# Probabilities times values in four tiles of TensorE: 64 keys against the 96 queries that see them

## The chip, the cores and the metric

The kernel runs on one core of one Trainium2 chip. The metric is the device time of one execution in microseconds (us). The time before is the median of three runs.

## The reference

A windowed attention is followed by a gated MLP. There are 8 batches and 8 heads, 576 positions and 64 numbers per head. Heads 0 to 3 see the last 32 positions (plain), heads 4 to 7 every fourth of the last 128 (dilated).

```python
scores = scale * np.matmul(q, k.transpose(0, 1, 3, 2))
rel = pos[:, None] - pos[None, :]
mask_plain = (rel >= 0) & (rel < window)                                        # window = 32
mask_dil = (rel >= 0) & (rel < window * dilation) & (rel % dilation == 0)       # dilation = 4
scores = np.where(masks[None, :, :, :], scores, -1000000000.0)
attn = np.exp(scores - np.max(scores, axis=-1, keepdims=True))
attn = attn / (np.sum(attn, axis=-1, keepdims=True) + 1e-09)
attn_out = np.matmul(attn, v)                   # (8, 8, 576, 64)
...
h = x @ w_in                                    # x: (4608, 512), w_in: (512, 2048)
g = h * (1.0 / (1.0 + np.exp(-1.702 * h)))
return g @ w_out                                # w_out: (2048, 512)
```

## The kernel before, in words

**Pairs.** Two heads of one batch make a pair, 32 pairs `k` in all, four to a batch (the first two plain, the last two dilated). The dilated heads' positions are sorted by their remainder by 4, so that in both kinds a query sees only the 32 positions before and with it. Pairs 0 to 3 have a path of their own (`first_product`). Pairs 4 to 31, 28 of them, go through `attention`: the change is there.

**One pair.** `scores` (L480) multiplies blocks of 32 queries by 64 keys in tiles of TensorE of 64 rows and 32 columns, head `a` in row group `a`, into the two banks of the PSUM tile `sp`, columns 0 to 319 of each. VectorE adds the mask (`add_mask`; for pairs below 8 TensorE does it), takes maxima and sums; ScalarE takes exponentials; GpSimd or VectorE divides by the sums. VectorE transposes blocks of 32 by 32 into `ct` (L531). Eight copies (L540 to L545, on ScalarE or VectorE, by DMA for pairs 4 to 7) lay the blocks out in `bt`, whose zeros are written once at L1180. `product` multiplies them by the values `v`; `drain_x` copies the result from PSUM to `xm`, `arena` and, for positions 512 to 575, to `rests_x`.

**The product before.** For each of nine blocks of 64 queries and each of the two heads, one matmul takes the 96 keys that the block can see (`bt` of 96 partitions, `v` of 96 by 64) and writes 64 queries. Head `a` writes to partitions 64 `a` and up, so that two column tiles are in use. Queries 0 to 511 go to the tile `av`, the last 64 to columns 320 to 383 of the second bank of the `sp` tile that holds the next pair's scores (`rest`). For pairs 24 and up a tile `sp` of its own holds both.

**The MLP.** Groups 0 to 2 (512 tokens each, one batch) run `up` (L821, into the one bank `hp_m`), a tanh on ScalarE (L829), a product on VectorE (L830), which frees `hp_m`, a split into a high and a low half (`gh`, `gl`), and `Down.pieces` (L758 to L762, `acc_m`). The other six groups run as three blocks `p`, `q`, `r` (L964, L1079) with sums of weights and tokens instead. Every matmul there is 128 by 128 by 512.

**The order.** Nothing is ordered by hand: the steps are handed to `Plan` with a cost per engine, with what they read and write (`"sp"`, `"left"`, `"av"` and so on) and an urgency. `Plan.placed` lists them engine by engine from these costs, and where a step may run on two engines it picks one. Each engine then runs its list in that order. When a cost changes, the list changes in places that are far from it too. A product is one step of TensorE; if it is `joint`, the next pair's scores stand ahead of it in the same step. DMAs are issued from the queue of SP.

**Helpers.** Copies all run at L338 (ScalarE) or L340 (VectorE), sums and differences of two tensors at L345, so that tiles tell them apart.

Of the kernel before, what the change touches and what calls it, by code (L numbers as in the profile page):

```python
# [34 lines left out]
W = 64  # L35
NW = 9
KW = 96
ROW = S // 4
INNER = 24
# [176 lines left out]
def tile_windowed_attention_then_gated_mlp(  # L216
# [41 lines left out]
    ghs, gls = ([fixed([P, GT], F32R, f"{n}{j}") for j in range(2)] for n in ("gh", "gl"))  # L258
    bt = fixed([P, 2, NW + 1, D], F32, "bt")
    arena = fixed([P, NU, GT], F32, "arena")  # L260
# [22 lines left out]

    cts = [fixed([P, 2, 2, QT, 32], F32, f"ct{j}") for j in range(2)]

    third = area(13, 3)
    prs.append(third[:, 0:2 * QT * W].rearrange("p (a t w) -> p a t w", a=2, t=QT))
    cts.append(third[:, 2 * QT * W:4 * QT * W].rearrange("p (h a t q) -> p h a t q", h=2, a=2, t=QT))

# [36 lines left out]
    def mask_dilated():  # L326

        A.activation(mask, plain, AF.Copy)
        G.affine_select(out=mask[0:32, 1, 0:48], in_=mask[0:32, 1, 0:48], pattern=[[0, 48]], compare_op=ALU.is_ge,
                        fill=NEG, base=15, channel_multiplier=-1)  # L330
        V.memset(mask[32:64, 1, 0:16], NEG)
        V.memset(mask[32:64, 2, 0:32], NEG)
        A.activation(mask[32:64, 3], mask[0:32, 1], AF.Copy)
        V.memset(mask[64:96, 3, 0:16], NEG)

# [15 lines left out]
    def decode(n, urgency):  # L351
# [21 lines left out]
        def fetch(e):  # L373
            if n == 3:
                raw = bt.rearrange("p a n w -> p (a n w)")[:, 0:2 * DM].bitcast(U64)
            else:
                raw = temp([P, DM], U64, "qk", f"cell_{n}") if n == 4 else cells[r]
            at["halves"] = raw.bitcast(U16).rearrange("p (n t) -> p n t", t=4)
            at["low"], at["top"] = (raw.bitcast(U32).rearrange("p (n t) -> p n t", t=2)[:, :, j] for j in range(2))
            load(raw, src)  # L380
# [21 lines left out]
    late, main_x, left_x = area(0, 4), area(9, 4), left  # L402
    nv = NW * D
    pairs = [{} for _ in range(B * NC)]
# [23 lines left out]
    def load_v(k):  # L428
        u, place = pairs[k], lots(k)[1]

        def work(e):
            if k < NC:
                n = (QT if dilated(k) else QT + 1) * 2 * D
                flat = (None, late, main_x, left_x)[k][:, 2 * S:2 * S + n] if k else temp([P, n], F32, "v", f"v_{k}")
                u["v"] = flat.rearrange("p (s a d) -> p s a d", a=2, d=D)

                load(flat, first_v[k][:, 2 * D * (QT + 1) - n:])
                return
            flat = temp([P, 2 * nv], F32, "v", f"v_{k}")
            u["v"] = [flat[:, nv * a:nv * a + nv].rearrange("p (m d) -> p m d", m=NW) for a in range(2)]  # L440
            for a in range(2):
                load(u["v"][a][0:KW], vp[k - NC, :, a])

        add({DMA: 390 if k < NC else 442}, (-6.7, -6.7, -3.8, -1.6)[k] if k < NC else 1.6 * k - 0.3, work, waits(k),
            (place, place + "l"), (0.0, 4.0, 11.0, 14.0)[k] if k < NC else 0.0)
# [15 lines left out]
    def scores(k):  # L461
# [8 lines left out]
        for t in range(QT):  # L470
            for a, g in [(a, g) for a in range(2) for g in range(4 if k < NC or t < QT - 1 else 2)]:
                rows = slice(D * a, D * a + D)
                dst = u["box"][a][32 * g:32 * g + 32, t]
                at = ROW * g + 32 * t if k < NC else P * t + 32 * g

# [36 lines left out]
    def softmax(k, urgency):  # L512
# [10 lines left out]
        if k < NC:  # L523

            for a in range(2):
                to = ct.rearrange("p h a t q -> p (h a t q)")[:, a * QT * W:a * QT * W + QT * W]
                add({DVE: 0.48}, urgency, lambda e, a=a, to=to: V.transpose(
                    out=to, in_=pr[:, a].rearrange("p t w -> p (t w)")), (PR, f"{PR}.{a}"), (f"{CT}.{a}",))
            return
        for half in (0, 1):  # L530
            add({DVE: 0.42}, urgency, lambda e, half=half: V.transpose(  # L531
                out=ct[:, half], in_=pr[:, :, :, 32 - 32 * half:64 - 32 * half]),
                (PR, f"{PR}.0", f"{PR}.1"), (f"{CT}.{half}",))
# [3 lines left out]
        for m in range(8):  # L537
            j, prev = m % 4, m // 4
            row = 32 * (j % 2) + (0 if prev else 32)
            dst = bt[row:row + 32, :, j // 2::2, 32 * (j % 2):32 * (j % 2) + 32]  # L540
            src = ct[32 * j:32 * j + 32, prev]

# [9 lines left out]
    def first_product(k):  # L552
# [4 lines left out]
        u = pairs[k]  # L557
        ct = cts[turn(k)].rearrange("p h a t q -> p (h a t q)").rearrange("p (a n) -> p a n", a=2)
        u["x"] = first_x[:, :, ROW * (k % 2):ROW * (k % 2) + ROW]
# [13 lines left out]
    def product(k):  # L573
        u = pairs[k]
        if k < INNER:
            u["av"] = bank([P, GT], "av", f"av_{k}")
            n = following(k)
            sp = pairs[n]["sp"] if n else bank([P, 2, GT], "sp", f"rest_{k}")
            u["rest"] = sp[:, 1, QT * W:QT * W + LT]
        else:  # L580
            sp = bank([P, 2, GT], "sp", f"av_{k}")
            u["av"], u["rest"] = sp[:, 0], sp[:, 1, 0:LT]
        for m in range(NW):
            for a in range(2):
                rows = slice(D * a, D * a + D)
                dst = u["av"][rows, D * m:D * m + D] if m < NW - 1 else u["rest"][rows]
                T.matmul(dst, u["v"][a][0:KW, m], bt[0:KW, a, m], start=True, stop=True, skip_group_check=True)

    def drain_x(k, urgency):
# [7 lines left out]

        if dilated(k) and b:
            def whole():
                return u["av"][:, 0:432].rearrange("p (r i) -> p r i", r=3)  # L600
            mains = [(384, lambda x: x[:, 0:3], lambda: whole()[:, :, 0:P], False),
                     (80, lambda x: x[:, 3, 0:80], lambda: u["av"][:, 432:512], False),
                     (48, lambda x: x[:, 3, 80:P], lambda: u["rest"][:, 0:48], True)]
            rests = [(lambda x: x[:, 0:3], lambda: whole()[:, :, P:], False),
                     (lambda x: x[:, 3], lambda: u["rest"][:, 48:], True)]
        else:
            mains = [(GT, lambda x: x, lambda: u["av"], False)]
            rests = [(lambda x: x, lambda: u["rest"], True)]
        if b == 0:
# [26 lines left out]
        if b >= ALONE:  # L636
            add({DMA: 262}, urgency, lambda e: load(tokens_x[k], to), [f"{name}.{n}" for n in range(3)], (f"tx{k}",))
        for n, (part, src, other) in enumerate(rests):
# [5 lines left out]
    def store_rest(b, c, urgency):  # L644
        if c < NC - 1:
            return
        y = 1 - b % 2
        dst = tokens_r.rearrange("c p (b n) -> b p c n", b=B)[b]
        add({DMA: 66}, urgency, lambda e: load(dst, rests_x[:, y]), [f"xr{y}{i}.{n}" for i in range(NC) for n in range(2)],
            (f"tr{b}",))  # L650

    def parts(k):
        return 3 if dilated(k) else 1

# [10 lines left out]
    def attention(k, urgency):  # L665
# [25 lines left out]
        def work(e):  # L691
# [5 lines left out]
        places = ("sp",) if k >= INNER else ("left", "av", "sp") if joint else ("left", "av")  # L697
        add({PE: 2.2 if joint else 1.25}, urgency - 1.0e5, work,
            (lots(k)[1], *(f"bt.{m}" for m in range(8)), *need), places, 1.0)
# [12 lines left out]
    def unit(i):  # L712
        if i < NU:
            return arena[:, i]
        if i >= NU + 4:
# [6 lines left out]
            if n >= 8:  # L722
                return bt.rearrange("p a n w -> p (a n w)")[:, GT * (n - 8):GT * (n - 7)]
            if n < 6:
                return prs[n - 4].rearrange("p a t w -> p (a t w)")[:, 0:GT]
            return cts[n - 6].rearrange("p h a t q -> p (h a t q)")[:, 0:GT]
        if "wi_last" not in misc:
# [62 lines left out]
    class Group:  # L790
# [366 lines left out]
    for i, name in enumerate(("qk0", "qk0", "v0", "v0", "pr0", "pr1", "ct0", "ct1")):
# [106 lines left out]
```

## Time and profile before

| what | value |
|---|---|
| median of three runs | 838.21 us (837.95 to 838.41) |
| profiled execution | 835.92 us, span 834.2 us |
| mean granted clock of TensorE | 0.993 |
| first and last record of the changed product (L587) | 71.8 and 472.0 us |
| DMA, whole span | 191.47 MB, mean 230 GB/s |

The span runs from the first to the last instruction; the rest of an execution lies outside. Line numbers are those of the kernel before. In the profile an f32 matmul of the program is two records on PE and two weight loads on PEld. The shape behind a matmul (96\*64, 64\*32) is the rows and columns of its tile. Ends of matmul records are modelled, so their starts are what is read.

### The profile page before, as it was taken

Reading aid. Unit: us, or ns where it says so; the run is one execution under the profiler, and the core shown is the slowest. Engines: PE = TensorE matmul, PEld = TensorE weight load, DVE = VectorE, ACT = ScalarE, POOL = GpSimd, SP = SyncE. Lnnn points to the kernel's source line nnn. Section 1 sums busy time; section 2 is a strip of 40 time slices with the busy share of each in tenths; the row PEclk is TensorE's granted clock in tenths of the full one; section 3 lists DMA queues with packets and bytes.
Section 4 is the critical chain, followed back from the end, with each engine's and each line's share of the span. In section 5 each row is a group of like instructions: output and inputs, shape, how many; then the busy total and the mean of one; then the engine's idle time right before and its main releaser. Section 6 shows DMA issues by size and latency. Waiting matters only on the chain. (4 is left out here: it accounts for less than half of the span.)

```text
span 834.2 us, 18369 instructions
## 1 busy us (share of the span) xinstructions
PE 817.4 (98%) x7016; PEld 659.3 (79%) x7016; DVE 682.0 (82%) x1104; ACT 521.5 (63%) x936; POOL 331.2 (40%) x296
## 2 busy tenths in 40 slices
PE   7899999999999999999999999999999999999997
PEld 4578887888887888787888887888888888888886
DVE  6898999878889977887988999886678976767575
ACT  7898876776777666767765764445446544544340
POOL 3443235566754565234322463541125431112251
PEclk9899999999999999999999999999999999999999
DMA  9477659999867747859777877685655658665546
GB/s 359 144 250 221 196 155 301 297 294 315 272 216 249 231 153 235 285 191 320 245 235 253 252 251 243 218 272 178 208 182 192 202 190 264 227 187 170 200 144 185
DMA packets 113128, 191.47 MB, mean 230 GB/s; under 512 B 28176, under 2 KB 57104, under 8 KB 113040
## 3 DMA queue, kind: packets, MB, share of 16 engines
q1 hardware_dynamic: 112896, 190.16, 70.2%
q8 instruction: 56, 0.92, 0.5%
q14 instruction: 32, 0.26, 0.1%
q10 hardware_dynamic: 144, 0.13, 0.0%
HBM read 143.85 MB, written 45.09 MB: 226 GB/s over the span
## 5 line engine op out<-in xcount | busy, mean ns | idle before, releaser
L345 POOL TENSOR_TENSOR arena<-arena 128x256 f32<-128x256 f32 (+3 forms) x102 | 108.8, 1072 | 118.2 <-DVE wi_last_units L345 23.0
L821 PE MATMUL hp_m<-xs,wi_kept 128*128 128x512 f32 x504 | 129.2, 398 | 1.5 <-DVE arena L830 1.0
L821 PEld LDWEIGHTS hp_m<-xs,wi_kept 128*128 128x128 f32 x504 | 92.8, 188 | 24.0 <-DVE arena L830 3.1
L338 ACT ACTIVATE wo_kept<-arena 128x512 fp32r<-128x512 f32 x111 | 69.4, 630 | 41.9 <-PE second_r_Q L1079 10.0
L964 PE MATMUL up_r<-wi_kept,xs 128*128 128x512 f32 x336 | 85.4, 389 | 0.0
L964 PE MATMUL up_p<-wi_kept,xs 128*128 128x512 f32 x336 | 85.0, 395 | 0.2 <-DVE arena L986 0.2
L964 PE MATMUL up_q<-wi_kept,xs 128*128 128x512 f32 x336 | 83.5, 389 | 0.3 <-DVE arena L986 0.3
L345 POOL TENSOR_TENSOR wo_kept<-arena,wo_kept 128x512 fp32r<-128x512 f32 x32 | 43.0, 1349 | 93.2 <-ACT wo_kept L338 50.9
L964 PEld LDWEIGHTS up_q<-wi_kept,xs 128*128 128x128 f32 x336 | 63.0, 188 | 13.8 <-DVE arena L986 0.7
L964 PEld LDWEIGHTS up_p<-wi_kept,xs 128*128 128x128 f32 x336 | 62.0, 188 | 14.5 <-DVE arena L986 0.6
L964 PEld LDWEIGHTS up_r<-wi_kept,xs 128*128 128x128 f32 x336 | 63.1, 188 | 13.1
L345 DVE TENSOR_TENSOR wo_kept<-arena,wo_kept 128x512 fp32r<-128x512 f32 x89 | 67.8, 770 | 6.4 <-ACT wo_kept L338 5.8
L345 POOL TENSOR_TENSOR wo_kept<-wi_last_units,wo_kept 128x512 fp32r<-128x512 f32 x25 | 34.7, 1388 | 94.7 <-ACT wo_kept L338 90.3
L338 ACT ACTIVATE bt<-ct 32x320 f32<-32x320 f32 x124 | 58.2, 469 | 14.2 <-DVE ct L531 10.4
L345 POOL TENSOR_TENSOR pr<-pr,sm 128x320 f32<-128x320 f32 x52 | 43.7, 857 | 54.6 <-DVE sm L510 45.2
L758 PE MATMUL acc_m<-gh,wo_kept 128*128 128x512 f32 x156 | 61.4, 394 | 0.3 <-ACT arena L338 0.3
L759 PE MATMUL acc_m<-gh,wo_kept 128*128 128x512 f32 x156 | 60.8, 389 | 0.0
L985 ACT ACTIVATE arena<-arena 128x512 f32<-128x512 f32 x60 | 37.5, 629 | 34.8 <-DVE arena L345 28.8
L345 DVE TENSOR_TENSOR arena<-arena 128x512 f32<-128x512 f32 (+1 forms) x71 | 55.3, 780 | 1.3 <-ACT arena L338 0.9
L345 DVE TENSOR_TENSOR gl<-arena,gh 128x512 fp32r<-128x512 f32 x54 | 46.7, 864 | 6.6 <-ACT gh L338 3.7
L338 ACT ACTIVATE wo_kept<-wi_last_units 128x512 fp32r<-128x512 f32 x48 | 30.2, 630 | 29.0 <-PE second_r_Z L1079 8.9
L338 ACT ACTIVATE gh<-arena 128x512 fp32r<-128x512 f32 x56 | 35.7, 637 | 17.8 <-DVE arena L830 6.1
(262 smaller groups left out, 1836.5 us busy)
## 6 DMA issues: line engine op xcount, KB each, us to landing
xs<-sums SPq DMA_DIRECT2D x168, 256.0 KB, 3.5
out_weights<-sums_o SPq DMA_DIRECT2D x63, 512.0 KB, 3.8
qk<-qk_dram SPq DMA_DIRECT2D x29, 576.0 KB, 4.8
v<-vp_dram SPq DMA_DIRECT2D x56, 216.0 KB, 4.2
xs<-sums_o SPq DMA_DIRECT2D x21, 512.0 KB, 3.7
sums<-arena SPq DMA_DIRECT2D x32, 256.0 KB, 3.7
sums_o<-arena SPq DMA_DIRECT2D x32, 256.0 KB, 3.6
arena<-wi_dram SPq DMA_DIRECT2D x15, 512.0 KB, 4.3
```

Of the source, the lines that this page charges most:

```text
L338: A.activation(dst, src, AF.Copy, scale=scale)
L345: (V if e == DVE else G).tensor_tensor(out=dst, in0=a, in1=b, op=op)
L758: T.matmul(self.acc[j], w[:, 0, cols], high, start=f == 0, stop=False)
L759: T.matmul(self.acc[j], w[:, 1, cols], high, start=False, stop=False)
L821: T.matmul(hps[f], wi(f)[:, st, cols], mv[:, c], start=c == 0 and k == 0, stop=c == NC - 1 and k == 2)
L964: T.matmul(self.banks[place], xs[:, slot, at:at + P], wi_kept[:, 2 * a + c, mv], start=fresh and c == 0 and k == 0, stop=c == 1 and k == 2 ...
L985: add({ACT: 0.60}, -10.0, lambda e: A.activation(unit(tmp), src(), AF.Tanh, scale=0.851), need, own(tmp))
```

## The change

- **Blocks.** Queries and keys are cut differently. A half is 320 positions, five blocks of 64; the first starts at position 0, the second at 256 for the keys. A block of 64 keys is multiplied by the up to 96 queries that see it. Lower keys (row group 0) hold the first half, upper keys (row group 1) the second, and each has two heads, so four tiles of 64 by 64.
- **Banks.** Each query is seen from two key blocks, so its two parts are added up in PSUM: only the first matmul to each bank and head has `start`. Row group 0 writes 320 columns of `av`. Row group 1 writes the 192 columns behind the scores in the first bank of `sp`, and the last 64 behind those of the second.
- **Drains.** A plain pair has two main copies and one of the rest, a dilated one five and three (before: one and one, three and two).
- **Values.** `v` is one transfer of 128 by 640 f32 instead of two of 96 by 576.
- **Around it.** The tiles of queries in `scores`, the masks, `ct` (tile ahead of head) and the eight copies to `bt` follow the new layout; five of these move 256 elements per partition and three 320 (before: eight of 320). The zeros are written over 128 by 960 instead of 96 by 1280.
- **Plan's costs.** TensorE's step is given as 1.95 and 1.05 instead of 2.2 and 1.25, the load of `v` as 328 instead of 442.

```diff
-NW = 9
+NB = 5
 KW = 96
+HALF = 2 * NB * 32
...
+    bt_all = fixed([P, 5 * 2 * P], F32, "bt")
+    bt = bt_all[:, 0:2 * NB * KW].rearrange("p (s a w) -> p s a w", a=2, s=NB)
...
-            flat = temp([P, 2 * nv], F32, "v", f"v_{k}")
-            u["v"] = [flat[:, nv * a:nv * a + nv].rearrange("p (m d) -> p m d", m=NW) for a in range(2)]
-            for a in range(2):
-                load(u["v"][a][0:KW], vp[k - NC, :, a])
+            flat = temp([P, 2 * NB * D], F32, "v", f"v_{k}")
+            u["v"] = flat.rearrange("p (a s d) -> p a s d", a=2, s=NB)
+            load(flat, vp[k - NC])
...
-                at = ROW * g + 32 * t if k < NC else P * t + 32 * g
+                at = ROW * g + 32 * t if k < NC else HALF * (g // 2) + W * t + 32 * (g % 2)
...
-                out=ct[:, half], in_=pr[:, :, :, 32 - 32 * half:64 - 32 * half]),
+                out=ct[:, half].rearrange("p t a q -> p a t q"), in_=pr[:, :, :, 32 - 32 * half:64 - 32 * half]),
...
-            row = 32 * (j % 2) + (0 if prev else 32)
-            dst = bt[row:row + 32, :, j // 2::2, 32 * (j % 2):32 * (j % 2) + 32]
-            src = ct[32 * j:32 * j + 32, prev]
+            odd, upper = j % 2, j // 2
+            row = D * upper + 32 * (odd != prev)
+            col = 32 * odd if not prev or odd else 64
+            shift = prev and not odd
+            tiles = slice(1 if shift and not upper else 0, QT - upper)
+            to = slice(1, QT) if upper and not shift else slice(0, tiles.stop - tiles.start)
+            dst = bt[row:row + 32, to, :, col:col + 32]
+            src = ct[32 * j:32 * j + 32, prev, tiles]
...
-            u["rest"] = sp[:, 1, QT * W:QT * W + LT]
+            u["x"] = u["av"][:, 0:HALF], sp[:, 0, QT * W:], sp[:, 1, QT * W:QT * W + LT]
...
-            u["av"], u["rest"] = sp[:, 0], sp[:, 1, 0:LT]
-        for m in range(NW):
-            for a in range(2):
-                rows = slice(D * a, D * a + D)
-                dst = u["av"][rows, D * m:D * m + D] if m < NW - 1 else u["rest"][rows]
-                T.matmul(dst, u["v"][a][0:KW, m], bt[0:KW, a, m], start=True, stop=True, skip_group_check=True)
+            u["x"] = sp[:, 0, 0:HALF], sp[:, 1, 0:GT - HALF], sp[:, 1, GT - HALF:S - HALF]
+        begun = set()
+        for m in range(NB):
+            for r in range(2):
+
+                n = KW if m < NB - 1 else W
+                if r == 0:
+                    spans = [(0, n, 0, W * m)]
+                elif m == 0:
+                    spans = [(W, KW, 1, 0)]
+                elif m < NB - 2:
+                    spans = [(0, n, 1, W * (m - 1))]
+                else:
+                    spans = [(0, W, 1, P), (W, KW, 2, 0)] if m == NB - 2 else [(0, W, 2, 0)]
+                for first, last, i, at in spans:
+                    bank_ = i if k < INNER else min(i, 1)
+                    for a in range(2):
+                        rows, keys = slice(D * a, D * a + D), slice(D * r, D * r + D)
+                        T.matmul(u["x"][i][rows, at:at + last - first], u["v"][keys, a, m], bt[keys, m, a, first:last],
+                                 start=(bank_, a) not in begun, stop=True, tile_position=(D * r, D * a),
+                                 skip_group_check=True)
+                        begun.add((bank_, a))
...
+        if dilated(k):
+            mains = [(2 * P, lambda y: y[:, 0:2], lambda: two(x(0, 0, 2 * ROW))[:, :, 0:P], 0),
+                     (32, lambda y: y[:, 2, 0:32], lambda: x(0, 2 * ROW, HALF), 0),
+                     (96, lambda y: y[:, 2, 32:P], lambda: x(1, 0, 96), 1),
+                     (80, lambda y: y[:, 3, 0:80], lambda: x(1, 112, 192), 1),
+                     (48, lambda y: y[:, 3, 80:P], lambda: x(2, 0, 48), 1)]
+            rests = [(lambda y: y[:, 0:2], lambda: two(x(0, 0, 2 * ROW))[:, :, P:], 0),
+                     (lambda y: y[:, 2], lambda: x(1, 96, 112), 1), (lambda y: y[:, 3], lambda: x(2, 48, LT), 1)]
         else:
-            mains = [(GT, lambda x: x, lambda: u["av"], False)]
-            rests = [(lambda x: x, lambda: u["rest"], True)]
+            mains = [(HALF, lambda y: y[:, 0:HALF], lambda: x(0, 0, HALF), 0),
+                     (GT - HALF, lambda y: y[:, HALF:], lambda: x(1, 0, GT - HALF), 1)]
+            rests = [(lambda y: y, lambda: x(2, 0, LT), 1)]
...
-        add({PE: 2.2 if joint else 1.25}, urgency - 1.0e5, work,
+        add({PE: 1.95 if joint else 1.05}, urgency - 1.0e5, work,
...
-            add({POOL: 1.2}, 20.0, lambda e: G.memset(bt[0:KW], 0.0), (), ("bt", "btl", *zeroed))
+            add({POOL: 1.2}, 20.0, lambda e: G.memset(bt, 0.0), (), ("bt", "btl", *zeroed))
```

More of the change, by code (lines that the diff above doesn't have):

```diff
@@ L258, in tile_windowed_attention_then_gated_mlp @@
     ghs, gls = ([fixed([P, GT], F32R, f"{n}{j}") for j in range(2)] for n in ("gh", "gl"))
-    bt = fixed([P, 2, NW + 1, D], F32, "bt")
+    bt_all = fixed([P, 5 * 2 * P], F32, "bt")
+    bt = bt_all[:, 0:2 * NB * KW].rearrange("p (s a w) -> p s a w", a=2, s=NB)
     arena = fixed([P, NU, GT], F32, "arena")
@@ L282, in tile_windowed_attention_then_gated_mlp @@
     sms = [fixed([P, 2, QT], F32, f"sm{j}") for j in range(3)]
-    cts = [fixed([P, 2, 2, QT, 32], F32, f"ct{j}") for j in range(2)]
+    cts = [fixed([P, 2, QT, 2, 32], F32, f"ct{j}") for j in range(2)]
     third = area(13, 3)
     prs.append(third[:, 0:2 * QT * W].rearrange("p (a t w) -> p a t w", a=2, t=QT))
-    cts.append(third[:, 2 * QT * W:4 * QT * W].rearrange("p (h a t q) -> p h a t q", h=2, a=2, t=QT))
+    cts.append(third[:, 2 * QT * W:4 * QT * W].rearrange("p (h t a q) -> p h t a q", h=2, a=2, t=QT))
     four = tc.tile_pool(name="four", bufs=1, space=bass.MemoryType.PSUM)
@@ L328, in mask_dilated @@
         A.activation(mask, plain, AF.Copy)
-        G.affine_select(out=mask[0:32, 1, 0:48], in_=mask[0:32, 1, 0:48], pattern=[[0, 48]], compare_op=ALU.is_ge,
+        G.affine_select(out=mask[0:32, 2, 0:48], in_=mask[0:32, 2, 0:48], pattern=[[0, 48]], compare_op=ALU.is_ge,
                         fill=NEG, base=15, channel_multiplier=-1)
[L331 to L334, printed above, removed]
+        V.memset(mask[32:64, 2, 0:16], NEG)
+        V.memset(mask[32:64, 4, 0:32], NEG)
+        A.activation(mask[96:128, 1], mask[0:32, 2], AF.Copy)
+        V.memset(mask[64:96, 2, 0:16], NEG)
     def copy(e, dst, src, scale=1.0):
@@ L374, in fetch @@
             if n == 3:
-                raw = bt.rearrange("p a n w -> p (a n w)")[:, 0:2 * DM].bitcast(U64)
+                raw = bt_all[:, 0:2 * DM].bitcast(U64)
             else:
@@ L402, in tile_windowed_attention_then_gated_mlp @@
     late, main_x, left_x = area(0, 4), area(9, 4), left
-    nv = NW * D
     pairs = [{} for _ in range(B * NC)]
@@ L438, in work @@
                 return
-            flat = temp([P, 2 * nv], F32, "v", f"v_{k}")
-            u["v"] = [flat[:, nv * a:nv * a + nv].rearrange("p (m d) -> p m d", m=NW) for a in range(2)]
-            for a in range(2):
-                load(u["v"][a][0:KW], vp[k - NC, :, a])
-        add({DMA: 390 if k < NC else 442}, (-6.7, -6.7, -3.8, -1.6)[k] if k < NC else 1.6 * k - 0.3, work, waits(k),
+            flat = temp([P, 2 * NB * D], F32, "v", f"v_{k}")
+            u["v"] = flat.rearrange("p (a s d) -> p a s d", a=2, s=NB)
+            load(flat, vp[k - NC])
+        add({DMA: 390 if k < NC else 328}, (-6.7, -6.7, -3.8, -1.6)[k] if k < NC else 1.6 * k - 0.3, work, waits(k),
             (place, place + "l"), (0.0, 4.0, 11.0, 14.0)[k] if k < NC else 0.0)
@@ L525, in softmax @@
             for a in range(2):
-                to = ct.rearrange("p h a t q -> p (h a t q)")[:, a * QT * W:a * QT * W + QT * W]
+                to = ct.rearrange("p h t a q -> p (h t a q)")[:, a * QT * W:a * QT * W + QT * W]
                 add({DVE: 0.48}, urgency, lambda e, a=a, to=to: V.transpose(
@@ L557, in first_product @@
         u = pairs[k]
-        ct = cts[turn(k)].rearrange("p h a t q -> p (h a t q)").rearrange("p (a n) -> p a n", a=2)
+        ct = cts[turn(k)].rearrange("p h t a q -> p (h t a q)").rearrange("p (a n) -> p a n", a=2)
         u["x"] = first_x[:, :, ROW * (k % 2):ROW * (k % 2) + ROW]
@@ L596, in view, with x, two @@
             return x.rearrange("p (i r) -> p r i", r=4) if dilated(k) and b else x
[L598 to L605, printed above, removed]
-        else:
-            mains = [(GT, lambda x: x, lambda: u["av"], False)]
-            rests = [(lambda x: x, lambda: u["rest"], True)]
+        def x(i, first, last):
+            return u["x"][i][:, first:last]
+        def two(ap):
+            return ap.rearrange("p (r i) -> p r i", r=2)
+        if dilated(k):
[6 more added lines that the diff above has]
+                     (lambda y: y[:, 2], lambda: x(1, 96, 112), 1), (lambda y: y[:, 3], lambda: x(2, 48, LT), 1)]
+        else:
+            mains = [(HALF, lambda y: y[:, 0:HALF], lambda: x(0, 0, HALF), 0),
+                     (GT - HALF, lambda y: y[:, HALF:], lambda: x(1, 0, GT - HALF), 1)]
+            rests = [(lambda y: y, lambda: x(2, 0, LT), 1)]
         if b == 0:
@@ L636, in drain_x @@
         if b >= ALONE:
-            add({DMA: 262}, urgency, lambda e: load(tokens_x[k], to), [f"{name}.{n}" for n in range(3)], (f"tx{k}",))
+            add({DMA: 262}, urgency, lambda e: load(tokens_x[k], to), [f"{name}.{n}" for n in range(5)], (f"tx{k}",))
         for n, (part, src, other) in enumerate(rests):
@@ L648, in store_rest @@
         dst = tokens_r.rearrange("c p (b n) -> b p c n", b=B)[b]
-        add({DMA: 66}, urgency, lambda e: load(dst, rests_x[:, y]), [f"xr{y}{i}.{n}" for i in range(NC) for n in range(2)],
+        add({DMA: 66}, urgency, lambda e: load(dst, rests_x[:, y]), [f"xr{y}{i}.{n}" for i in range(NC) for n in range(3)],
             (f"tr{b}",))
-    def parts(k):
-        return 3 if dilated(k) else 1
     def first_attention(k, urgency):
@@ L722, in unit @@
             if n >= 8:
-                return bt.rearrange("p a n w -> p (a n w)")[:, GT * (n - 8):GT * (n - 7)]
+                return bt_all[:, GT * (n - 8):GT * (n - 7)]
             if n < 6:
                 return prs[n - 4].rearrange("p a t w -> p (a t w)")[:, 0:GT]
-            return cts[n - 6].rearrange("p h a t q -> p (h a t q)")[:, 0:GT]
+            return cts[n - 6].rearrange("p h t a q -> p (h t a q)")[:, 0:GT]
         if "wi_last" not in misc:
@@ L803, in split_x @@
                 x = xm[:, c]
-                need = [f"xm{c}.{n}" for n in range(parts(c))]
+                need = [f"xm{c}.{n}" for n in range(5)]
                 add({ACT: 0.53}, -8.0, lambda e, hi=hi, x=x: copy(e, hi, x), need, (f"xh{c}",))
@@ L1145, in tile_windowed_attention_then_gated_mlp @@
     for c in range(NC):
-        legacy[9 + c] = tuple(f"xm{c}.{n}" for n in range(3)) + ("first v2", "first qk2")
+        legacy[9 + c] = tuple(f"xm{c}.{n}" for n in range(5)) + ("first v2", "first qk2")
         legacy[13 + c] = ("first v3", "first qk3")
@@ L1150, in tile_windowed_attention_then_gated_mlp @@
             legacy[13 + c] += tuple(f"{n}2{i}" for n in ("pr", "ct") for i in ("", ".0", ".1")) + ("mx2",)
-    legacy[16] = tuple(f"xr{y}{c}.{n}" for y in range(2) for c in range(NC) for n in range(2))
+    legacy[16] = tuple(f"xr{y}{c}.{n}" for y in range(2) for c in range(NC) for n in range(3))
     legacy[17] = ("g32",)
@@ L1155, in tile_windowed_attention_then_gated_mlp @@
     for i in (8, 9):
-        legacy[i] += tuple(f"A{i}.{n}" for n in range(3))
+        legacy[i] += tuple(f"A{i}.{n}" for n in range(5))
     for i, name in enumerate(("qk0", "qk0", "v0", "v0", "pr0", "pr1", "ct0", "ct1")):
@@ L1243 @@
     first = np.ascontiguousarray(first.reshape(NC, 2, 4, QT + 1, 32, D).transpose(0, 2, 4, 3, 1, 5))
-    vp = np.stack([vp[:, :, D * m:D * m + KW] for m in range(NW)], axis=2)
-    vp = np.ascontiguousarray(vp.reshape(B * NC, 2, NW, KW, D).transpose(0, 3, 1, 2, 4))
+    vp = np.stack([vp[:, :, 32 + first:32 + first + HALF] for first in (0, S - HALF)], axis=2)
+    vp = vp.reshape(B * NC, 2, 2, NB, W, D).transpose(0, 2, 4, 1, 3, 5)
+    vp = np.ascontiguousarray(vp).reshape(B * NC, P, 2 * NB * D)
     wi = np.asarray(inputs["moe_w_in"]).view(np.uint64).reshape(NC, P, NF, P).transpose(2, 1, 0, 3)
```

## The prediction

> **What bounds the kernel now.** I read the page first, then the busy time by stage, then what TensorE waits for in the stages that hold the change, and last the order of time around one product.
>
> ```profile
> span 834.2 us, 18369 instructions
> PE 817.4 (98%) x7016; PEld 659.3 (79%) x7016; DVE 682.0 (82%) x1104; ACT 521.5 (63%) x936; POOL 331.2 (40%) x296
> ```
>
> TensorE is busy for 98% of the span. A busy TensorE need not be at its peak, so the stages come next (columns: window, its length, then busy time and count of PE, PEld, DVE, ACT and POOL, the granted clock, the DMA share, GB/s).
>
> ```profile
> 18.00:71.00 53.00, 48.81 (x650) 36.22 (x651) 47.02 (x85) 47.52 (x74) 23.55 (x22) 0.92 0.60 193
> 71.00:125.00 54.00, 54.00 (x561) 43.21 (x561) 51.40 (x87) 46.18 (x77) 14.55 (x13) 1.00 0.69 205
> 125.00:225.00 100.00, 98.99 (x1326) 79.39 (x1326) 85.77 (x144) 70.66 (x138) 64.08 (x64) 1.00 0.91 297
> 225.00:325.00 100.00, 99.73 (x1181) 81.33 (x1176) 84.57 (x146) 69.97 (x142) 57.48 (x62) 1.00 0.65 207
> 325.00:425.00 100.00, 98.87 (x918) 79.08 (x916) 85.57 (x145) 72.57 (x138) 31.91 (x27) 1.00 0.79 263
> 425.00:475.00 50.00, 50.00 (x392) 40.56 (x379) 43.12 (x75) 32.67 (x68) 18.27 (x15) 1.00 0.78 252
> 475.00:834.00 359.00, 353.82 (x1555) 291.00 (x1553) 273.72 (x399) 168.87 (x287) 115.80 (x82) 1.00 0.64 207
> ```
>
> All 28 changed products lie between 71 and 475 us. There TensorE is busy 401.6 of 404 us at clock 1.00, VectorE 350.4 and ScalarE 292.1. The waits of TensorE in that window are few:
>
> ```profile
> PE hp_m L821 <- DVE arena L830: 2.0, 4, 1.0
> PE acc_m L758 <- ACT arena L338: 0.3, 1, 0.3
> PE up_p L964 <- DVE arena L986: 0.2, 1, 0.2
> ```
>
> That is 2.5 us in 404. So a microsecond less for TensorE there is close to a microsecond of the kernel, as long as the others keep up; after 475 us it is again TensorE (353.8 of 359).
>
> **The product, removed and added.** One joint step in order of time, TensorE alone (start, length, line, what, count), and one lone product:
>
> ```profile
> 158.94 0.97 PE L480 MATMUL sp<-qk 64*32 64x64 f32 x72
> 159.84 1.15 PE L587 MATMUL av<-bt,v 96*64 96x64 f32 x32
> 160.82 0.29 PE L587 MATMUL sp<-bt,v 96*64 96x64 f32 x4
> 161.04 2.33 PE L821 MATMUL hp_m<-xs,wi_kept 128*128 128x512 f32 x9
> ...
> 470.96 1.27 PE L587 MATMUL av<-bt,v 96*64 96x64 f32 x36
> 472.16 0.73 PE L964 MATMUL up_p<-wi_kept,xs 128*128 128x512 f32 x2
> ```
>
> An f32 matmul of the program shows as two records, which I call halves. A product is 18 matmuls, 36 halves, and holds TensorE from its first half to the next work: 161.04 - 159.84 = 1.20 us, and 472.16 - 470.96 = 1.20 us. The last six halves to `av` start from 160.65 on, the first to `sp` at 160.82:
>
> ```profile
> 160.65 0.35 PE L587 MATMUL av<-bt,v 96*64 96x64 f32 x6
> ```
>
> So two heads in two column tiles take one step of 0.17 / 3 = 0.057 us for a half each; over the whole, 32 halves in 0.98 us with the start, I use 0.058. With 18 steps per tile, 17 intervals make 0.99, and 1.20 - 0.99 = 0.21 us is start and drain.
>
> What makes the step? Windows at the beginning of the scores (PE and PEld with counts of records that fall in each) show it:
>
> ```profile
> 158.93:158.99 0.06, 0.05 (x8) 0.05 (x12) 1.00 0.43 154
> 158.99:159.02 0.03, 0.03 (x8) 0.03 (x16) 1.00 0.19 68
> 159.02:159.09 0.07, 0.07 (x18) 0.07 (x26) 1.00 0.22 73
> ...
> L480 PEld LDWEIGHTS sp<-qk x2100: 102/106/173, 5.4 to 441.1; 64*32 64x32 f32 x191
> L821 PEld LDWEIGHTS hp_m<-xs,wi_kept x504: 186/188/333, 26.9 to 330.3; 128*128 128x128 f32 x168
> L587 PEld LDWEIGHTS av<-bt,v x928: 132/138/138, 71.8 to 472.0; 96*64 96x64 f32 x186
> ```
>
> The first eight halves start at once, one in each of eight tiles of 64 rows and 32 columns; no half starts between 158.99 and 159.02, while weight loads go on; the ninth comes 0.08 us after the first. A weight load grows by (188 - 106) / 96 = 0.85 ns per column, so 32 columns are 0.027 and the 64-wide stream behind them about 0.053, or 0.83 ns per query. Two things follow. Tiles of two row groups and several column groups run beside each other, each at its own pace. And a half of 96 queries should take 96 x 0.83 = 0.080 plus the 0.005 that the step of 0.058 has over its 0.053: 0.085 us. A half of 64 or 32 queries keeps 0.058, since its weights still have 64 columns (64 x 0.85 = 0.054).
>
> The new product has 22 matmuls, 44 halves. On TensorE, the product of pair 9 and its neighbours; `av` and `sp` are PSUM tiles, `bt` the probabilities, `v` the values, `hp_m` the MLP. Before:
>
> ```order
> L480 MATMUL sp_12_2098<-qk_12_2027 32x64 x36
> L587 MATMUL av_9_2135<-bt_77,v_9_2030 64x64 x16
> L587 MATMUL sp_12_2098<-bt_77,v_9_2030 64x64 x2
> L821 MATMUL hp_m1_4_2094<-xs_72,wi_kept_68 128x512 x9
> L758 MATMUL acc_m1_3_1949<-gh0_73,wo_kept_70 128x512
> ```
>
> And now:
>
> ```order
> L482 MATMUL sp_12_2120<-qk_12_2048 32x64 x36
> L607 MATMUL av_9_2157<-bt_77,v_9_2052 64x96 x2
> L607 MATMUL sp_12_2120<-bt_77,v_9_2052 64x32 x2
> L607 MATMUL av_9_2157<-bt_77,v_9_2052 64x96 x2
> L607 MATMUL sp_12_2120<-bt_77,v_9_2052 64x96 x2
> L607 MATMUL av_9_2157<-bt_77,v_9_2052 64x96 x2
> L607 MATMUL sp_12_2120<-bt_77,v_9_2052 64x96 x2
> L607 MATMUL av_9_2157<-bt_77,v_9_2052 64x96 x2
> L607 MATMUL sp_12_2120<-bt_77,v_9_2052 64x64 x2
> L607 MATMUL sp_12_2120<-bt_77,v_9_2052 64x32 x2
> L607 MATMUL av_9_2157<-bt_77,v_9_2052 64x64 x2
> L607 MATMUL sp_12_2120<-bt_77,v_9_2052 64x64 x2
> ```
>
> The lower 64 keys go to `av`, the upper 64 to `sp`, two heads each: four tiles. A lower tile has 8 halves of 96 and 2 of 64: its nine intervals are 8 x 0.085 + 0.058 = 0.74. An upper tile has 4 of 32, 4 of 96 and 4 of 64: eleven intervals, 4 x 0.085 + 7 x 0.058 = 0.75, and it starts two issue slots later (0.01). With the same 0.21 for start and drain a product takes 0.97 us. Gain: 0.23 a product, **28 x 0.23 = 6.4 us**. The bounds: if the weight load alone sets every step, 11 x 0.058 + 0.22 = 0.86, a gain of 9.5 us; if the four tiles go key block by key block, each block as slow as its slower tile (three of 0.17, then four halves of 0.058, then two, less the last interval: 0.80), 1.02, a gain of 5.0. I take 6.4, since the tiles of the scores do not wait for each other. Issue is no limit: the first product of pair 3 sends 80 halves over eight tiles in 35.38 - 34.37 = 1.01 us, 0.013 each, and 44 of them make 0.56.
>
> ```profile
> 34.37 1.08 PE L568 MATMUL first_x<-ct,arena 32*64 32x64 f32 x80
> 35.38 0.50 PE L821 MATMUL hp_m<-xs,wi_kept 128*128 128x512 f32 x1
> ```
>
> **The other edits.** The drains are cut finer, since the result now lies in three stretches. A plain pair has one more copy, a dilated one three more.
>
> ```profile
> L338 ACT ACTIVATE arena<-av x59: 198/371/875, 73.0 to 473.2; 128x512 f32<-128x512 f32 x14, 128x384 f32<-128x384 f32 x14, 128x80 f32<-128x80 f32 x14, 128x48 f32<-128x48 f32 x10
> L338 ACT ACTIVATE arena<-sp x21: 200/253/312, 73.5 to 321.2; 128x48 f32<-128x48 f32 x10, 128x16 f32<-128x16 f32 x6, 128x64 f32<-128x64 f32 x5
> ...
>   DVE pr L345: 1.5, 3
> ...
> L338 ACT ACTIVATE bt<-ct x124: 454/470/475, 151.2 to 467.9; 32x320 f32<-32x320 f32 x124
> ```
>
> At 0.20 to 0.31 us for a small copy, 14 + 3 x 14 = 56 more copies are 11 to 17 us, fewer as the large ones shrink. Five of the eight copies into `bt` fall from 320 to 256 elements: between nothing and a fifth of 0.47 us each, 0 to 11 us over 24 pairs. ScalarE so gets between nothing and 17 us more work, in 404 us of which it idles 112. VectorE's transposes keep their count and size and only write in another layout; I cost that at nothing, under the 54 us that VectorE idles. The values come as one transfer of 327 KB in place of two of 216 KB; TensorE waits for none of them now, so I cost that at nothing, and at nothing too if the cover went, as the new transfer is smaller. The planner, given shorter costs, also lays the whole program out anew.
>
> What I do charge is one new kind of wait. The `sp` tile holds the next pair's scores, which VectorE reads, and now also 192 + 64 columns of the product, not 64. ScalarE already waits for VectorE's mask addition there, 1.5 us in three times (the row `DVE pr L345` above, of what ended the idle time before the copies out of `sp`).
>
> On ScalarE behind the product of pair 10 (`bt`, `av`, `sp` as above, `hp_m` the tanh, `pr` the exponentials, `gh` the gate). Before:
>
> ```order
> L338 ACTIVATE arena_78<-av_10_2272 128x3x128
> L338 ACTIVATE bt_77<-arena_78 32x10x32 x8
> L829 ACTIVATE arena_78<-hp_m1_6_2301 128x512
> L338 ACTIVATE arena_78<-av_10_2272 128x80
> L338 ACTIVATE arena_78<-sp_13_2235 128x48
> ```
>
> And now:
>
> ```order
> L342 ACTIVATE arena_78<-sp_13_2264 128x96
> L856 ACTIVATE arena_78<-hp_m1_6_2331 128x512
> L342 ACTIVATE arena_78<-sp_13_2264 128x80
> L342 ACTIVATE arena_78<-sp_13_2264 128x48
> L342 ACTIVATE arena_78<-av_10_2301 128x32
> L506 ACTIVATE pr1_84<-pr1_84 128x640
> ```
>
> A copy out of `sp` now stands ahead of the tanh. Whoever delays it delays the tanh, then VectorE's L830, then the next `hp_m`. The present cost of that path is the 2.0 us above; I add **0.6 us**, a guess between -1.5 (the new layout loses most of the waits of now) and +4 (it doubles them and more).
>
> Sum: -6.4 + 0.6 = -5.8 us. The profiled execution took 835.92 us (span 834.2), so 830.1; the median of the runs is 838.21, 2.29 above it, so **832.4 us**.
>
> **The rivals.**
> Waits eat the gain (slower). VectorE adds the masks in two pieces, 0.69 and 0.27 us; if ScalarE stands before that in each of the 20 pairs from 4 to 23 and half of the 0.96 reaches `hp_m`, that is 20 x 0.5 = 10 us, and 838.2 - 6.4 + 10 = 842. It decides once the delay exceeds what TensorE has in hand, the 12 matmuls of the down part (one every 0.22, 2.6 us) less tanh and L830 (0.60 and 0.69). For it: VectorE is at 86% there, and ScalarE's eight `bt` copies make 3.9 us in one piece. Against: 1.3 us in hand each time, and only four waits of now reach TensorE.
>
> ```profile
> L829 ACT ACTIVATE arena<-hp_m x48: 574/598/703, 39.3 to 346.0; 128x512 f32<-128x512 f32 x48
> L830 DVE SCALAR_TENSOR_TENSOR arena<-arena,hp_m x48: 630/687/690, 40.6 to 347.0; 128x512 f32<-128x512 f32 x48
> ...
> 157.72 0.39 PE L758 MATMUL acc_m<-gh,wo_kept 128*128 128x512 f32 x1
> 157.94 0.39 PE L759 MATMUL acc_m<-gh,wo_kept 128*128 128x512 f32 x1
> ...
> 172.26 3.85 ACT L338 ACTIVATE bt<-arena 32x320 f32<-32x320 f32 x8
> L345 DVE TENSOR_TENSOR arena<-sp,mask x6: 272/474/692, 150.7 to 283.6; 128x512 f32<-128x512 f32 x3, 64x128 f32<-64x128 f32 x3
> ```
>
> The tiles take turns (slower). If halves start only in program order, the second half of a matmul holds up the next tile, and each of the 22 matmuls costs one step: 12 x 0.085 + 10 x 0.058 + 0.21 = 1.81, +0.61 a product, +17 us: 855. Against it stand the scores: 36 matmuls in 159.84 - 158.94 = 0.90 us, where turns of 0.058 would need 2.1. [...]
>
> Half the gain: blocks in step (5.0) with +2 to +3 of waits, or 6.4 with +4: 835 to 836.3. And the weight load sets all steps: 838.2 - 9.5 + 0.6 = 829.3.
>
> **How the numbers follow.** Four tiles at their own pace with waits about as now: 0.68, which is the forecast. Half the gain: 0.15. Weight load: 0.04. Waits eat all of it and no more: 0.05. Waits eat more: 0.04; turns: 0.04. A measurement of this kernel tells 0.2% (1.7 us) from no change, so faster has 0.68 + 0.15 + 0.04 = 0.87, same 0.05, slower 0.08. The range goes from the weight-load case, 829.3, to the upper end of half the gain, 836.3; it leaves out some 0.17.
>
> **What would show it.** Right: a product from first half to next work at 0.94 to 1.02 us, 44 halves; TensorE's waits between 71 and 475 us under 5 us; everything after the last product about 6 us earlier. Wrong: a product at 1.2 us or more (turns), or `hp_m` waiting for L830 by 6 us or more, with ScalarE's copies out of `sp` waiting for the mask additions.

## The result and the profile after

| | before | changed |
|---|---|---|
| median | 837.95 us (836.90 to 838.41, 5 runs) | 830.17 us (828.89 to 830.57, 5 runs) |
| profiled execution | 835.92 us, span 834.2 us | 828.89 us, span 827.2 us |
| product, first half to next work | 1.20 us | 0.955 us |
| last product: next work starts at | 472.16 us | 465.37 us |

The ratio is 0.9905 (95% interval 0.9891 to 0.9920): 7.8 us faster, 6.7 to 9.1 by the interval. The forecast was 832.4 us in a range of 829.3 to 836.3. Line numbers are now those of the changed kernel: L607 is the product, L482 the scores, L856 the tanh and L857 VectorE's step behind it.

The page after, and the stages between 71 and 475 us and behind (columns as before):

```profile
span 827.2 us, 18837 instructions
PE 811.2 (98%) x7240; PEld 653.5 (79%) x7240; DVE 669.7 (81%) x1104; ACT 515.0 (62%) x992; POOL 327.8 (40%) x296
...
71.00:125.00 54.00, 53.91 (x602) 42.25 (x608) 47.75 (x84) 47.15 (x92) 16.73 (x14) 1.00 0.64 198
125.00:225.00 100.00, 99.40 (x1423) 80.04 (x1423) 85.27 (x151) 65.65 (x143) 62.24 (x65) 1.00 0.87 288
225.00:325.00 100.00, 99.88 (x1229) 80.70 (x1223) 80.51 (x144) 72.49 (x167) 54.04 (x59) 1.00 0.64 211
325.00:425.00 100.00, 98.41 (x915) 78.84 (x920) 88.07 (x147) 71.34 (x148) 31.81 (x28) 1.00 0.79 253
425.00:475.00 50.00, 49.35 (x468) 39.87 (x455) 44.52 (x73) 33.48 (x76) 21.81 (x19) 1.00 0.81 262
475.00:827.00 352.00, 347.10 (x1528) 286.18 (x1526) 265.73 (x394) 163.90 (x277) 112.08 (x79) 1.00 0.64 206
```

TensorE's share stays at 98%. It is busy for 98% or more of each of these stages, so it still sets the time there, and its busy time fell by 6.2 us. What it waits for between 71 and 475 us:

```profile
PE up_p L991 <- DVE arena L349: 1.3, 2, 0.7
PE up_p L991 <- DVE arena L1013: 0.9, 1, 0.9
PE acc_m L785 <- ACT arena L342: 0.3, 1, 0.3
PE hp_m L848 <- DVE arena L857: 0.2, 1, 0.2
```

2.7 us against 2.5 before, in other places: `hp_m` waits 0.2 us for VectorE, not 2.0. The product of pair 9 in order of time, TensorE alone (start, length, what, count; two halves start together, 0.007 us apart, which I read as one for each head):

```profile
157.84 0.30 PE L607 MATMUL av<-bt,v 64*64 64x96 f32 x2
157.85 0.30 PE L607 MATMUL sp<-bt,v 64*64 64x32 f32 x4
157.97 0.25 PE L607 MATMUL av<-bt,v 64*64 64x96 f32 x2
157.99 0.28 PE L607 MATMUL sp<-bt,v 64*64 64x96 f32 x2
158.05 0.25 PE L607 MATMUL av<-bt,v 64*64 64x96 f32 x2
158.10 0.25 PE L607 MATMUL sp<-bt,v 64*64 64x96 f32 x2
158.13 0.25 PE L607 MATMUL av<-bt,v 64*64 64x96 f32 x2
158.18 0.25 PE L607 MATMUL sp<-bt,v 64*64 64x96 f32 x2
158.22 0.25 PE L607 MATMUL av<-bt,v 64*64 64x96 f32 x2
158.26 0.25 PE L607 MATMUL sp<-bt,v 64*64 64x96 f32 x2
...
158.64 0.22 PE L607 MATMUL sp<-bt,v 64*64 64x64 f32 x2
158.79 0.50 PE L789 MATMUL acc_m<-gl,wo_kept 128*128 128x512 f32 x1
```

A lower tile starts a half of 96 queries every 0.08 us (157.97, 158.05, 158.13, 158.22), and an upper tile does the same in between: four tiles run beside each other. From 157.84 to 158.79 the product takes 0.95 us. So do 27 of the 28; behind one, at 168.16 us, the next work waits 0.2 us for VectorE (the `hp_m` row above). The last product, of pair 31, says the same:

```profile
464.42 1.02 PE L607 MATMUL av<-bt,v 64*64 64x96 f32 x44
465.37 0.73 PE L991 MATMUL up_p<-wi_kept,xs 128*128 128x512 f32 x2
```

Up to there the profiled execution is 472.16 - 465.37 = 6.8 us ahead; at the end it is 7.0. The products give 28 x (1.198 - 0.955) = 6.8 us.

### The profile page after: what moved, and what is told of

It is laid out like the page before. It is cut to its first block, busy times and chain, and to the rows that moved or that the text cites. A ratio compares the mean times of both kernels' runs of the same rounds, so it can differ in the third digit from the quotient of the medians.

```text
span 827.2 us, 18837 instructions
## 1 busy us (share of the span) xinstructions
PE 811.2 (98%) x7240; PEld 653.5 (79%) x7240; DVE 669.7 (81%) x1104; ACT 515.0 (62%) x992; POOL 327.8 (40%) x296
## 4 chain that ended last, share of the span: by engine, by line
PE 88%; DVE 7%; ACT 1%; issue 1%; DMA 1%; SPq 0%; DVEq 0%; ACTq 0%
PE hp_m L848 15%; PE up_q L991 9%; PE up_r L991 9%; PE up_p L991 8%; PE second_q_Q L1106 5%; PE second_r_Q L1106 5%; PE second_p_Q L1106 5%; PE acc_m L785 5%; PE acc_m L789 5%; PE acc_m L786 4%; PE sp L482 3%; PE second_r_Z L1106 3%; PE second_R L1106 3%; PE second_q_Z L1106 3%; PE second_p_Z L1106 2%; PE av L607 2%
## 5 line engine op out<-in xcount | busy, mean ns | idle before, releaser
L349 POOL TENSOR_TENSOR arena<-arena 128x256 f32<-128x256 f32 (+3 forms) x109 | 118.0, 1091 | 155.7 <-DVE wi_last_units L349 34.7
L342 ACT ACTIVATE wo_kept<-arena 128x512 fp32r<-128x512 f32 x115 | 71.9, 629 | 42.3 <-PE second_r_Q L1106 11.4
L349 POOL TENSOR_TENSOR wo_kept<-arena,wo_kept 128x512 fp32r<-128x512 f32 x34 | 45.3, 1340 | 105.5 <-ACT wo_kept L342 72.2
L349 DVE TENSOR_TENSOR wo_kept<-arena,wo_kept 128x512 fp32r<-128x512 f32 x87 | 65.3, 761 | 5.9 <-ACT wo_kept L342 5.4
L349 POOL TENSOR_TENSOR wo_kept<-wi_last_units,wo_kept 128x512 fp32r<-128x512 f32 x23 | 31.9, 1388 | 84.6 <-ACT wo_kept L342 84.6
L342 ACT ACTIVATE bt<-ct 32x256 f32<-32x256 f32 (+1 forms) x127 | 55.2, 435 | 3.2 <-DVE ct L533 0.9
L349 DVE TENSOR_TENSOR gl<-arena,gh 128x512 fp32r<-128x512 f32 x53 | 44.9, 847 | 9.1 <-PE acc_m L789 6.4
L349 DVE TENSOR_TENSOR arena<-arena 128x512 f32<-128x512 f32 (+1 forms) x68 | 50.4, 747 | 0.4
L1013 DVE SCALAR_TENSOR_TENSOR arena<-arena 128x512 f32<-128x512 f32 x60 | 48.1, 807 | 0.7 <-ACT arena L1012 0.2
```

Of the source, the lines that this page charges most:

```text
L342: A.activation(dst, src, AF.Copy, scale=scale)
L349: (V if e == DVE else G).tensor_tensor(out=dst, in0=a, in1=b, op=op)
L1013: add({DVE: -0.70 if need[0][0] == "A" else 0.70}, -10.0, lambda e: V.scalar_tensor_tensor(out=unit(dst), in0=unit(tmp), scalar=1.0, in1=s ...
```

## The experiments

Each was timed in rounds with the kernel before on the same chip; the medians of before were 837.39, 837.62 and 837.71 us in the three sets.

**The plan's costs of before in the changed kernel.**

```diff
-        add({PE: 1.95 if joint else 1.05}, urgency - 1.0e5, work,
+        add({PE: 2.2 if joint else 1.25}, urgency - 1.0e5, work,
...
-        add({DMA: 390 if k < NC else 328}, (-6.7, -6.7, -3.8, -1.6)[k] if k < NC else 1.6 * k - 0.3, work, waits(k),
+        add({DMA: 390 if k < NC else 442}, (-6.7, -6.7, -3.8, -1.6)[k] if k < NC else 1.6 * k - 0.3, work, waits(k),
```

> The changed kernel with the plan's costs of before (2.2 and 1.25 for TensorE's step, 442 for the load of the values); the work is the same, only the order of the lists may differ. Tiles theory (the gain is TensorE's time in the product, 28 x 0.243 = 6.8 us, and nothing else): the product stays at 0.955 us and the time at 830.2 us, give or take 1.5 for the other order. Plan theory (a part of the gain is the new order that the new costs made): 833 us or more with the same product.

830.25 us (ratio 0.9918, 0.9896 to 0.9940), product 0.955 us. That is 7.1 us less than the kernel before on the same chip (5.0 to 8.7 by the interval): most of the gain, if not all, does not need the new costs.

**The plan's new costs alone, in the kernel before.** The same two edits the other way round.

> The kernel before with the plan's costs of the change (1.95 and 1.05, 328) and nothing else of it. Tiles theory: the product stays at 1.198 us and the time at 838 us, give or take 1.5. Plan theory: 835 us or less, with the old product.

835.43 us (ratio 0.9976, 0.9965 to 0.9986), product 1.198 us. Neither theory had this: a new order alone made the kernel before 2.0 us faster.

**Other costs in the kernel before.**

```diff
-        add({PE: 2.2 if joint else 1.25}, urgency - 1.0e5, work,
+        add({PE: 2.1 if joint else 1.2}, urgency - 1.0e5, work,
```

> The kernel before with the plan's costs of TensorE's step at 2.1 and 1.2 (what its trace shows) instead of 2.2 and 1.25. The product stays at 1.198 us. Scatter theory (a new order moves the time by up to 2 us either way, without a trend): 835.5 to 839 us. If the costs of before were simply too high, so that lower ones gain: near 835.4 us, as with 1.95 and 1.05.

839.27 us (ratio 1.0023, 1.0011 to 1.0035), a touch above the stated band: 1.6 us slower, with costs of TensorE's step that lie between those of before and the new ones (the cost of loading `v` stays at 442 here). These two tries show no trend with the cost. A new order of the same work moved the kernel before by 2.0 us one way and by 1.6 the other.

**Measured costs in the changed kernel.**

```diff
-        add({PE: 1.95 if joint else 1.05}, urgency - 1.0e5, work,
+        add({PE: 1.85 if joint else 0.95}, urgency - 1.0e5, work,
```

> The changed kernel with the plan's costs of TensorE's step set to what the trace shows: 0.90 + 0.955 = 1.85 joint and 0.95 alone instead of 1.95 and 1.05. The work is the same and only the order of the lists differs. Tiles theory: 830 us give or take 2, the scatter of a new order. Plan theory: better costs make a better order, 828 us or less.

830.85 us (ratio 0.9917, 0.9901 to 0.9933), product 0.955 us. Costs nearer to the truth gain nothing that these runs resolve.

**Lower keys first, then upper keys.**

```diff
-        for m in range(NB):
-            for r in range(2):
+        for r in range(2):
+            for m in range(NB):
```

> The changed kernel with the loops of the product turned round: first all ten matmuls of the lower keys (row group 0, two tiles), then all twelve of the upper keys. Same matmuls, same banks. If each tile has a deep queue of its own, the product stays at 0.955 us and the time at 830 us. If TensorE looks only a short way ahead of what it has started, the upper tiles start when the lower ones are nearly done: up to 0.77 + 0.79 + 0.15 = 1.7 us a product, +21 us, 851 us.

844.57 us (ratio 1.0089, 1.0070 to 1.0108), product 1.500 us: between the two. One product in order of time:

```profile
150.54 0.80 PE L607 MATMUL av<-bt,v 64*64 64x96 f32 x14
151.10 0.25 PE L607 MATMUL sp<-bt,v 64*64 64x32 f32 x2
151.17 0.25 PE L607 MATMUL av<-bt,v 64*64 64x96 f32 x2
151.18 0.34 PE L607 MATMUL sp<-bt,v 64*64 64x32 f32 x4
151.26 0.28 PE L607 MATMUL av<-bt,v 64*64 64x64 f32 x4
151.35 0.76 PE L607 MATMUL sp<-bt,v 64*64 64x96 f32 x18
152.04 0.50 PE L848 MATMUL hp_m<-xs,wi_kept 128*128 128x512 f32 x1
```

From 150.54 on the lower tiles are at work, yet the first upper half starts at 151.10, 0.56 us later, as soon as 14 of the 20 lower halves have started and six are still to come. In this run TensorE thus did start halves of later matmuls ahead of earlier ones, but the upper ones not from the beginning. In the changed kernel (fence above) the first upper halves of 96 queries start at 157.99, when four of the lower halves that stand before them in the program are still to come.

**Two blocks of lower keys, then two of upper keys.**

```diff
-        for m in range(NB):
-            for r in range(2):
+        for blocks_ in ((0, 1), (2, 3), (4,)):
+            for r, m in [(r, m) for r in range(2) for m in blocks_]:
```

> The changed kernel with the matmuls of the product in another order: lower keys of blocks 0 and 1, upper keys of blocks 0 and 1, then blocks 2 and 3, then 4. In the run with the rows apart the upper tiles started when six halves of the lower ones were still to begin. If that is how far TensorE looks ahead, six halves are just what stands between here, the upper tiles start at once and the product stays at 0.955 to 1.0 us, 830 to 831.5 us. If it looks less far: 1.1 us or more a product, 834 us or more. If each tile simply has a pace of its own, 0.955 us.

832.48 us (ratio 0.9935, 0.9922 to 0.9948), product 1.053 us. The start came as expected, the rest did not:

```profile
148.93 0.30 PE L607 MATMUL av<-bt,v 64*64 64x96 f32 x2
148.96 0.30 PE L607 MATMUL sp<-bt,v 64*64 64x32 f32 x4
...
149.21 0.25 PE L607 MATMUL sp<-bt,v 64*64 64x96 f32 x2
149.23 0.33 PE L607 MATMUL av<-bt,v 64*64 64x96 f32 x4
149.32 0.30 PE L607 MATMUL sp<-bt,v 64*64 64x96 f32 x2
149.39 0.25 PE L607 MATMUL av<-bt,v 64*64 64x96 f32 x2
149.46 0.25 PE L607 MATMUL sp<-bt,v 64*64 64x96 f32 x2
```

The upper tiles start 0.03 us after the lower ones, past six halves of theirs. But their block 2 starts at 149.32, some 0.11 us after their last half of block 1 instead of 0.08, when the first halves of lower block 2 have just started: until then eight halves of lower blocks 2 and 3 stood ahead, now six are still to come. The step after it, to 149.46, is late too, at some 0.13 us, with only four halves ahead; why is not shown. These two late steps and the later start make the 0.1 us. The expectation had counted the six only at the start.

**Two key blocks sent twice.** Here the keys of the last two blocks count double in the sums.

```diff
-                for first, last, i, at in spans:
+                for first, last, i, at in spans * (2 if m > 2 else 1):
```

> The changed kernel with the matmuls of the last two of the five key blocks sent twice (these keys count double in the sums; the plan isn't told). That adds 0.28 us to a lower tile and 0.33 to an upper one, so a product takes 1.23 to 1.29 us, and 28 of them 7.8 to 9.2 us more. If TensorE's time in the product is the kernel's time one for one: 838.0 to 839.4 us. If other engines set the end in part of the stages: under 835 us.

841.38 us (ratio 1.0054, 1.0037 to 1.0072), product 1.403 us; both are more than expected:

```profile
150.27 0.25 PE L607 MATMUL sp<-bt,v 64*64 64x96 f32 x2
150.31 0.33 PE L607 MATMUL av<-bt,v 64*64 64x96 f32 x4
150.40 0.27 PE L607 MATMUL sp<-bt,v 64*64 64x64 f32 x2
...
150.98 0.34 PE L607 MATMUL sp<-bt,v 64*64 64x64 f32 x6
151.25 0.50 PE L848 MATMUL hp_m<-xs,wi_kept 128*128 128x512 f32 x1
```

At 150.40 the upper tiles are late again, 0.13 us after their last start instead of 0.08, this time with the doubled lower block ahead (eight halves, of which two have started), and at the end they run three steps alone. Six are left when they go on, as with the rows apart.

The same runs price TensorE's time. Each is set against a kernel with the product of 0.955 us on the same chip (830.25 with the old costs, 829.27 with two transfers). The rows apart cost 28 x 0.545 = 15.3 us of products and 844.57 - 830.25 = 14.3 of the kernel, the repeats 28 x 0.448 = 12.5 and 841.38 - 830.25 = 11.1, the pairs of blocks 28 x 0.098 = 2.7 and 832.48 - 829.27 = 3.2. So a microsecond of product is about one of kernel, 0.9 to 1.2, to within the 2 us that another order may bring. The third pair of numbers is hardly larger than that scatter; the first two carry the price.

**Every drain in two halves.**

```diff
-            add({ACT: 0.12 + size * 0.001}, urgency, lambda e, part=part, src=src: copy(
+            add({ACT: 0.12 + size * 0.001}, urgency, lambda e, part=part, src=src: copy_halves(
```

(The same in the copies of the rests; `copy_halves` calls `copy` for the first and the second half of the columns.)

> The changed kernel with every copy out of PSUM after a product cut in two halves; the plan isn't told. That is 14 x 3 + 14 x 8 = 154 more copies, each some 0.2 us of ScalarE or VectorE, about 31 us of work, nearly three times the 56 copies that the change added. Cover theory (the drains lie beside TensorE's work): 830 to 832 us, TensorE's waits between 71 and 475 us under 5 us. Waits theory (ScalarE late at the tanh, so that TensorE waits for hp_m): half of the added 0.6 to 1.6 us a pair would reach TensorE, some 15 us, 845 us.

829.81 us (ratio 0.9902, 0.9889 to 0.9915), product 0.955 us. What ended ScalarE's idle time before the copies out of `sp`, and TensorE's waits between 71 and 475 us:

```profile
L342 ACT ACTIVATE arena<-sp x106: 178/253/360, 74.0 to 324.1; 128x8 f32<-128x8 f32 x20, 128x48 f32<-128x48 f32 x20, 128x40 f32<-128x40 f32 x20, 128x24 f32<-128x24 f32 x20
...
  DVE pr L355: 1.3, 5
```

```profile
PE up_p L997 <- DVE arena L355: 1.3, 2, 0.7
PE up_p L997 <- DVE arena L1019: 0.9, 1, 0.9
PE hp_m L854 <- DVE arena L863: 0.3, 1, 0.3
PE acc_m L791 <- ACT arena L342: 0.3, 1, 0.3
```

With twice the copies TensorE waits 2.8 us, as in the changed kernel (2.7). The drains lie beside its work.

**The values in two transfers.**

```diff
-            load(flat, vp[k - NC])
+            for j in range(2):
+                n = NB * D
+                load(flat[:, n * j:n * j + n], vp[k - NC][:, n * j:n * j + n])
```

> The changed kernel with the values loaded by two transfers of 160 KB instead of one of 320 KB, 28 more issues on SP's queue. Nothing waits for them in the trace, so 830 us, within 1 us of the changed kernel. If the one transfer was part of the gain: 831.5 us or more, with TensorE waiting for it.

829.27 us (ratio 0.9899, 0.9885 to 0.9913). The one transfer is no part of the gain that the timing resolves.

**Upper keys first in each block.**

```diff
-            for r in range(2):
+            for r in (1, 0):
```

> The changed kernel with the upper keys ahead of the lower ones in each block. The upper tiles are the last to end (0.786 us from first to last start against 0.767), so starting them two slots of 0.0066 us sooner should end the product 0.01 us sooner: 0.942 us, 0.4 us in all, 829.8 us, which only the trace can show. If the order within a block matters more than that (the lookahead of six halves meets the 64 and 32 wide pair first): 0.98 us or more, 831 us.

829.62 us (ratio 0.9905, 0.9893 to 0.9918), and the product at 0.942 us as expected; the last one:

```profile
464.27 1.01 PE L607 MATMUL av<-bt,v 64*64 64x32 f32 x44
465.21 0.73 PE L991 MATMUL up_p<-wi_kept,xs 128*128 128x512 f32 x2
```

It is the shortest product of all. The 0.4 us that it should bring are below what the timing resolves, so that it beats the changed kernel is not shown.

## Why the prediction was right

- **What bounds it.** TensorE's time was the kernel's: three kernels with longer products paid 0.9 to 1.2 us for each microsecond, and of the 7.0 us that the span lost, the products make 6.8.
- **The product.** Forecast 0.97 us, measured 0.955. A half of 96 queries takes 0.082 us instead of 0.085, so the term is -6.8 us, not -6.4. The upper tile's chain is the longest, as forecast, and start and drain come out at about the 0.21 that was put in. The product lies between the two bounds of the forecast, 0.86 if the weight load set every step and 1.02 if the tiles went block by block. One detail is off: from the upper tile's last halves of 32 queries on, its steps are not 0.058 us each but 0.031, 0.058 and 0.086. Their sum is the same.
- **Tiles at a pace of their own.** Only half right, and luck that it didn't matter. In the change's order, lower and upper keys by turns, the first upper halves of 96 queries started with four lower halves still to come ahead of them (157.99), and from 158.10 on the upper tiles' steps of 96 came every 0.08 us. In the three kernels whose work stands in longer blocks upper halves started late, with six lower halves still to come ahead of them (151.10, 149.32 and 150.40), and the one with the same matmuls in two runs gave back the whole gain and more: 844.57 us. The forecast had no such delay; it held because of the order that the change happened to have.
- **The wait charged with +0.6 us.** It did not come: 2.7 us of waits against 2.5, and nearly three times the added copies cost nothing that shows. The reading was that a copy out of `sp` ahead of the tanh would delay `hp_m`. ScalarE, forecast with up to 17 us more work, has 290.1 us of it between 71 and 475 us against 292.1 before. That `hp_m` waits 0.2 us and not 2.0 may be the order's doing as much as the change's: with the same work in the orders that the old and the measured costs made it is 1.2 and 2.3.
- **Copies to `bt`, transfers of `v`, transposes.** The last two were costed at nothing. The transfer was tested and is nothing (the two of before were 221 KB each in the units of the 327, not 216). The transposes took as long as before, 0.498 us in the median then and 0.499 now. The copies to `bt` got shorter, by about an eighth where they move 256 elements, against 0.470 us before:

```profile
L342 ACT ACTIVATE bt<-ct x127: 412/417/473, 149.2 to 461.6; 32x256 f32<-32x256 f32 x76, 32x320 f32<-32x320 f32 x51
L533 DVE STREAM_TRANSPOSE ct<-pr x44: 463/499/511, 61.4 to 458.2; 128x320 f32<-128x320 f32 x44
```

Of these only the transfer was tried alone. The products leave 0.2 us of the span's 7.0 to all of them.
- **The new order.** The prediction spoke of the plan laying the program out anew but only priced waits between 71 and 475 us. Two new orders of the kernel before moved it by -2.0 and +1.6 us with no other change. This was the largest unknown, and the -1.0 us by which the medians moved beyond the products (7.8 against 6.8, within the interval) is of that size; that the order made it is not shown. Which waits make these 2 us is not settled: the profiled executions of the kernel before and of the one with the new costs have nearly the same span, 834.2 and 834.5 us.
- **The rivals.** Waits eat the gain: the waits did not grow, and the doubled copies speak against it. Half the gain: that needed a product of 1.02 us and 2 to 3 us more of waits, or 4 us more of waits, and neither came. The weight load sets all steps: the product would be 0.86 us. The tiles take turns: the product would be 1.8 us, which no run shows, and the second half of the first `av` matmul starts at 157.97, behind the `sp` halves at 157.85 that stand after it in the program.

## What to carry to other kernels

Price a small f32 matmul from the trace as the longer of its weight load and its stream of queries, for each tile, and take the longest tile's chain plus a fixed start and drain (0.2 us here); that gave 0.97 us for a measured 0.955. Let matmuls of different tiles alternate in the program: in the run with the rows apart most of the overlap was lost, 1.500 us for the same matmuls. And where a planner orders the whole program, give a change's forecast the scatter of a mere new order, which can be measured by altering a cost in the old kernel.

## What the runs showed of the hardware

TensorE started halves of f32 matmuls out of program order where their tiles differ: in the changed kernel the `sp` halves at 157.85 ahead of the second half of the first `av` matmul at 157.97. Where upper halves started late in the three kernels with longer blocks, six lower halves were still to come ahead of them (151.10, 149.32 and 150.40 us in the fences above); with two blocks at a time the step to 149.46 was late too, with four. Why is not shown. A half of 96 queries took 0.082 us with weights of 64 columns. Where the tiles' shape changes, 0.15 us passed from the last start of the product to the next work (158.64 to 158.79), against 0.06 between the lower tiles' last steps and 0.09 between the upper tiles'; how much of it the change of shape makes was not tried alone.
